# A retention layer and an MLP mixer in one kernel: the planner is given new durations, and the order and the engines of all steps are searched anew

## The chip, the cores and the metric

The kernel runs on one core of a Trainium2 chip. The metric is the time of one execution on the device in microseconds; of several runs the median is taken. Five engines work side by side: TensorE (PE, its weight loads shown apart as PEld), VectorE (DVE), ScalarE (ACT), GpSimd (POOL) and SyncE (SP). Each takes its instructions in the order in which the program lists them, and waits at an instruction until what it needs is there. Transfers are asked for by an engine (here GpSimd, SyncE and ScalarE) and then run on the DMA engines by themselves.

## The reference

```python
# q, k, v: (4, 8, 768, 64); B batches, H heads, S steps, D wide
gamma = 1.0 - 2.0 ** (-5.0 - np.arange(H))
for t in range(S):
    state = gamma * state + np.einsum('bhd,bhe->bhde', k[:, :, t], v[:, :, t])
    y[:, :, t] = np.einsum('bhd,bhde->bhe', q[:, :, t], state) / np.sqrt(D)
x = y.transpose(0, 2, 1, 3).reshape(B, S, H * D)                  # (4, 768, 512)
h = np.maximum(x.transpose(0, 2, 1) @ w_tok1, 0.0) @ w_tok2       # (768, 256), (256, 768)
u = x + h.transpose(0, 2, 1)
out = u + np.maximum(u @ w_ch1, 0.0) @ w_ch2                      # (512, 1536), (1536, 512)
```

## The kernel before

**The work.** A batch has four pairs of heads, and each pair goes through a *front* (`front`). Its k and q (loaded as fp16 by GpSimd's DMAs, L490 and L493) are scaled by powers of gamma (L531, L533) and turned, so that the head's width lies on the partitions: on TensorE (L555, L557, copied out at L565 and L570) for batches 0 and 1, by a DMA transpose from SyncE's queue (L545) for batches 2 and 3. A sequence is cut into six chunks of 128 steps. TensorE makes k by v of each chunk (L587), VectorE adds these up with decay (L599) and the result is scaled into `cross` (L617, L619). TensorE makes the scores of k and q (L638), VectorE masks them (L649, `am`), TensorE multiplies by v (L669) and adds what the earlier chunks give (L695). The sum leaves PSUM as x (L711), then follow the two token products (L726 with wt1, a relu at L735 or L737, L746 with wt2), whose result is added to x where it lies in PSUM, and leaves as u in fp16 and as X in fp32 (L711 twice). u is turned too (L791 and L797, or a DMA transpose).

Each batch then has a *back*: the product with wc1, a relu, the product with wc2, and the sum with X, which is stored (L1081, L983). Batch 0's first product is plain (`widen`, L825, L841). The others (`widen7`, L894; `narrow7`, L1042, L1052) multiply two by two blocks with seven products in place of eight; they need differences of blocks, which VectorE makes: of the weights once (`wsum` of wc2 at L1147, `AS` of wc1 at L1160, shown as `late`), of the activations each time (L864, L1006). Products that are used twice are kept in SBUF (`us`, L905, L1032), and the results come together at L914, L943 and L1059. The last blocks of batch 3 are done plainly in `narrow` (L968, L977).

**The order.** All this is 1246 steps, objects of `Op`, made in a fixed sequence and numbered so. A step has one or more *ways*: an engine, the time that it holds the engine, and the time until its result is there. Two strings written out in the kernel say what becomes of them. `ORDERED` lists all steps in the order of the plan, two characters for the number of each in base 62. `WAYS` has a digit for each step: which way it takes. From both each engine's own list follows, and that is what the engine is given. `arrange` walks through the lists with a model of the engines and the DMA rings (`Rings`, where `land` says how long after its last packet a transfer counts as landed), and gives each PSUM bank and buffer its place. The times of this walk aren't executed; they choose banks, and they decide how many *fillers* (matmuls of zeros, L1187, to keep TensorE running) stand between steps that are planned apart in the first 21 us. A search, outside the kernel, made the strings for these durations.

**Lists that the change touches.** GpSimd asks for q, k, v and the weights: wt1 (L473) as its step 11, the two halves of wt2 as 13 and 14, four parts of wc1 as 22, 23, 24 and 27, three parts of wc2 as 29 to 31. VectorE has the four sums of wc1 as steps 77, 87, 91 and 98, those of wc2 as 93 to 96, and batch 1's first mask as 66. The first pair's K comes in fp32 through SyncE, and both its halves are scaled on VectorE (L533). SyncE has 47 steps: one load, 26 DMA transposes and 20 stores; ScalarE issues the other stores.

Of the kernel before, what the change touches and what calls it, by code (L numbers as in the profile page):

```python
# [40 lines left out]
class Rings:  # L41
# [71 lines left out]
def arrange(ops, BANKS, seq, ways):  # L113
# [144 lines left out]

DIGITS = "0123456789abcdefghijklmnopqrstuvwxyzABCDEFGHIJKLMNOPQRSTUVWXYZ"
ORDERED = (  # L260
    "0d09060c070g010b000e0305080f1g0a1h0h1k0l1i1l0m1j0j1u1Q1v1R1y0i1w1U1x1S1V1T0n1m1n1z25241o280k2q1p272r1q0o2u1r"
    "262s1s1A291B0p1t342v2t1D350q1W1C1X2E1E1Y2F2H0v301Z2b20312G1F21322I222a2J0s1G23332d1H3e0u2c3h2w2e3g2x2f0w1I2y"
    "2z2K1J3f2A2B0r1L1K3j2L2C3i2g1M2D0t362h1N2M2N371O2O380x2i392P3k3a2l2j3b2Q1P3c0z3d5j2R4K2m0C2k483m3l493n3o2S2n"
    "2V3p4L0y4a2T3q2W2U0A2o3A3r2Y3B2p4b3v0B3s2Z3C5k3t3E2X0G4c3w3Fac3y3Daf0E3zai3xadaM4daeaNaPaQ3uaj0FagaYahauakav"
    "aZaO0Daxaw3Ob0aRaS3P0HaT3QayaUao3Saz3G3R4e3H4m4f3Ial4nap0I4g3JamaG4paqaHan3KaA1c0PaIaraD3LaE023MaB4has4iaCaJ"
    "4oatbd4qaKaF0Kbg4G4H4jb73NaLb14k1dbhbebi3Tbabmbf3U4l3W0Lbo3Vb43XbnaVb81f3Ybbb94rb2bcbp4Ib34tb50N184J3ZaW1940"
    "0Jbjb6bkaX1a41bO420M1bbl4443bq45bP1e4U464Mbrbx4v4V6m4Wbv4N5fbs4Obwby044P4s5g4Y4ubB0O4w4Q4Xbz4R0RbI4S5hbt4xbA"
    "4T5i0QbEbK5ObC50520T5P4y4ZbD6p51bT53c40S4z6nbFc8bU4A544C4BbX6qc54D6r5UbJc95l5V55bu4E5W5Rc7bM5m5X56bY5Scd5n5Y"
    "bN5o5a5T6U5Z5pbR5q60bQce5t6V5QbSbL575r5vch5s5u47bVci5x585y5w5AbWcm6o5bbZ5C5z5B0V6scn5Dc0c6596t5c5E6u616v5d6w"
    "c15Fcf6X6x4F6Y5e7s62cg7t5G646Z5J5Hcj635I65ca5K6W666y67ck695M5Lcb686b6a5N0X6A6ccl706z6E6d0U6Ccucq6ecI0Ycccwcv"  # L270
    "cr6icJ6f116Dcy6g6BcMczdCcs14cK6hcxcBcNcAct0WcCcPcLcOcQcDcG0Z71cW6jcRcEcHcU6kcFcS16cYcXcT6F6G6I72dD83127y736H"
    "cVcZd06JdG74157zd2d16KdIdHd37A75dJ7Bd46L7C7vdK7Dd5d86MdEdL76d6dFdOdMd7dPdodNd9da6N777w80787xdbdp6Q6O79de6R7b"
    "ds7udfdc7adqdt84dh6P7cdg859681dvdrdi7d7fdu8Bdwdj827e7h7gdmdx136SdA7idddkc28ydy17dlco7jdndzbGdB866l7kec7G7E97"
    "eged7F7o7Ieh7leeeE7m7H99el7K8C877L88dW7peF89em7N7Jencp9Eefepeo7n8a7Meyereq109adXeu8b8zez7O7Peiev7QeAeC7qesdQ"
    "7R7reDejdUet7S8Dek8edRdVeH8c8i8A7T8h8deJ8geI7U8f7W6TeLeK7XdS8k7Y8jdT7Z8leNeM8ndYeG8m8EeOc39ceBdZ989d8o9HeP9F"
    "eQ8F9ee0e19b8G7V9f8He3eR9ge2bH8p8Ie49heUe58q8JeVe88Ke68r8Le9eYe78s8MeZfc8N8tf28O8ufdf0f38Pfg8v8Qf5fh8xf19kf6"
    "eWfj8wfa9lew9GfefkeX8Rfb8Tfi9n8Vfo9mex9i8S8Uflf4fpfEff8Wfq9j9ofm8Xf7fnf88YfGfFf99qfsfH8ZfrfI90ftfufJ9pfv9K9I"
    "fL9Lfx9JfM9M9r9s9NfK919t92fy9OfwfN93fQfz9ufC95fO949PfRfAfDfSfP9veSfBfTg69wfWg79SfXga9W9xgb9UfZ9yfY9Tgdg09Vgc"
    "9zg4ge9Q9Xg8g1g5fU9Rg9gi9Agfgj9Yg2fV9Za0h2h6a1h4gga2goghhdh3h7h8hegGhbg3hhh5a3h9hcgqgHa4hihf9BgIa59DhggKhaa6"
    "hjhkgLhmgMgka8grgPgmhlgRglgQgpgvgna99CgSgtaba7gJgVgwgugTgNgWgxgsgUgOgzgygXgYgAgChogBhshGhphthIhqhHhuhwhvhKhx"  # L280
    "hygZhLhUhrhzhJhNhAiAgDhOhMhBgFi8eThPebhEaahChnhQgEhDhWhShRhViehFi9hYh0iahXhZicibhTi0i1idiCi2ifimi3igiGi6ihi4"
    "i7iki5iiioinijjAiliqiBisiriEiDjBipiFitjQiHiujeiIivjIiJjJiwiMixiyiNiKiziSiLjCjajKjLiOjfjDjcjEiPjMjliTjbiXiRiU"
    "jmiYiQjjjNjpjkiViZjdjOjnj0jPjqj1eajoh1jFjrj2j3jGjsj6iWjHj4jRjgj7j5j9jujSjhjxj8jvjYjTjijZjUjwjVjyk0k1k2jWjtk3"
    "jzk4jXk5"
)
WAYS = (
    "000000000000000000000000000000000000000000000000000000000000000000000000000000110000010000000000000000000000"
    "001000000000010000000000000000000100000100000000010000000000000000000000100001000100000000110000000000000000"
    "100101110100010000010000000000000000000011010000000000000000000000000100000100000000000100000000000000000000"
    "110000001000000000000000000000000001010000010000000000000000000000000000000000000000000000000010000000000100"  # L290
    "100100000000000000000000000000000110000000000000000000000000000011011000000000000000000000000000000001000100"
    "000000000000000000000000010000010000000000000001001000010000010001000000000000000010000000000000000000000000"
    "000000000000000000000000000000000000000000000000000000000000000000000000000011000000000000000000001100000000"
    "000000000000100000000000000000000000000000000000000000000000010000000000000000000000000000000000000000000000"
    "000000000000001100000000000000000000010000000000000000000010000000000000000000000000000000000000010000000000"
    "000000000001000001000000000000000010000000000000001000100000110000000000000000000001000000000010000000001100"
    "000000000000000000000000000000000000000000000100000000000100000000000001000000000000000000010000000000000001"
    "0000000000100010000100100000000001000000010000000000000001"
)


# [1 line left out]
def kernel(  # L303
# [22 lines left out]
    SH = S // 2  # L326
# [55 lines left out]
    def either(emit, **costs):  # L382
        return [(e, c[0], c[1], lambda emit=emit, e=e: emit(e)) for e, c in costs.items()]
# [98 lines left out]
    def load(b, p, what):  # L482
        src = dict(k=k, q=q, v=v)[what][b, 2 * p:2 * p + 2]
        hard = (b, p, what) in HARD
        wide = what == "q" and TURN[b, p, "q"] == "w"
        s = Slot("us" if hard else what)

        def emit():
            if wide:
                nc.gpsimd.dma_start(out=tile_of(s, [P, 2, NC, D], F16).rearrange("p h c d -> p h (c d)"),  # L490
                                    in_=src.rearrange("h (p c) d -> p h (c d)", c=NC))
            else:
                (nc.sync if hard else nc.gpsimd).dma_start(out=tile_of(s, [P, 2, NC, D], FP if hard else F16),  # L493
                                                           in_=src.rearrange("h (c p) d -> p (h c) d", p=P))
        dma = (96, 17) if hard else (16, 66) if wide else (96, 13.5)
        if hard:
            o = Op(ops, (-20, 0, b, p), [("SP", 500, 500, emit)], [], [s], dma=dma)
        else:
            o = request((-20, 0, b, p), 710 if wide else 1030, emit, dma, [s])
        loads[b, p, what] = (s, o)  # L500

    def front(b, p):
# [22 lines left out]
        def decayed(tag, src, dep, g, hard):  # L525
            dst, got = Slot(tag), []
            for j in range(2):
                def emit(e, j=j):
                    t, h = opened(dst, [P, NC, 2, D], F16)[:, :, j], 2 * p + j
                    if e == "ACT":  # L530
                        nc.scalar.activation(t, src.tile[:, j], AF.Copy, scale=g[:, h:h + 1])  # L531
                    else:
                        (nc.vector if e == "DVE" else nc.gpsimd).tensor_scalar(t, src.tile[:, j], g[:, h:h + 1], None,  # L533
                                                                               ALU.mult)
# [56 lines left out]
        prev = None  # L591
# [18 lines left out]
        if pair:  # L610
            rs = []
            for j in range(2):
                def emit(e, j=j):
# [3 lines left out]
                        nc.scalar.activation(r, u, AF.Copy, scale=g)  # L617
                    else:
                        nc.vector.tensor_scalar(r, u, g, None, ALU.mult)  # L619
                rs.append(op(either(emit, ACT=(455 + 115 * j, 555 + 40 * j), DVE=(465, 545)), [prev, cross_op] + rs, [] if j else [RS],  # L620
                             [RS, US] if j else [US]))
        else:
            rs = [op(either(emit, ACT=(455, 555), DVE=(305, 390)), [prev], [RS], [US])]
# [14 lines left out]
                nc.tensor.matmul(SC[g].tile[:, i * P:(i + 1) * P], KT.tile[rows, t], QT.tile[rows, t],  # L638
                                 start=True, stop=True)
# [165 lines left out]
    def back(b):  # L805
# [10 lines left out]
        def widen(sh):  # L816
            H2 = H2s[sh]
            rel = []
            for ft in range(NF):
# [17 lines left out]
                def emit(e, ft=ft, A=A, H2=H2):  # L837
# [382 lines left out]
```

## Time and profile before

| what | us |
|---|---|
| median of 3 runs | 186.37 |
| lowest and highest | 186.11, 187.1 |
| the profiled execution | 186.01 |
| its span, first to last instruction | 184.2 |

A page of the profile gives each engine's busy time as a share of the span, and the chain that ended last: from the last instruction back, at each step to what released it. A group's row names line, engine, operation, output and inputs, count, then busy time and mean nanoseconds of one, then the idle time ahead of it and what ended it. A row of a stretch gives the busy time of each engine in that stretch. A matmul's end is modelled and matmuls overlap, so TensorE's busy time says little by itself; the distance from one start to the next says more. The granted clock of TensorE was 0.998.

### The profile page before, as it was taken

The numbers are of one execution on the slowest core, as the hardware profiler recorded it, in microseconds if no ns is written. First come the engines' busy times: TensorE is split into PE (matmuls) and PEld (weight loads), VectorE is DVE, ScalarE is ACT, GpSimd is POOL, SyncE is SP. The second block draws the span as 40 slices with busy tenths as digits, with TensorE's granted clock in tenths as the row PEclk, the third lists the DMA queues.
The fourth block names the chain that finished last, engine by engine and source line by source line (L and its number), as shares of the span: only waits on it lengthen the run. The fifth ranks groups of instructions, "written<-read, shape, count | busy, mean of one in ns | idle before, by whom it ended". The sixth has DMA issues, their size and how long they took to land.

```text
span 184.2 us, 5242 instructions
## 1 busy us (share of the span) xinstructions
PE 176.4 (96%) x2087; PEld 134.1 (73%) x2087; DVE 166.0 (90%) x420; ACT 126.4 (69%) x295; POOL 53.6 (29%) x63
## 2 busy tenths in 40 slices
PE   7898999999999999999999999999999999999990
PEld 3465798566789788867669889677679986566880
DVE  5799899599999999999989999998999899779891
ACT  3858796659988999888998786989651516671000
POOL 8995776463409102595040200000000000000000
PEclk9999999999999999999999999999999999999999
DMA  6999999999999999999979998073400321700093
GB/s 109 155 172 179 188 177 201 179 194 206 167 156 142 157 110 159 137 149 155 136 143 243 207 141 205 30 197 33 113 0 4 101 43 68 278 0 0 4 342 115
DMA packets 94137, 25.31 MB, mean 137 GB/s; under 512 B 83616, under 2 KB 91296, under 8 KB 94112
## 3 DMA queue, kind: packets, MB, share of 16 engines
q0 software_dynamic: 67728, 13.18, 86.6%
q1 hardware_dynamic: 25232, 10.10, 26.9%
q10 hardware_dynamic: 1152, 1.70, 2.7%
q8 instruction: 16, 0.26, 0.6%
q14 instruction: 9, 0.07, 0.2%
HBM read 26.74 MB, written 6.29 MB: 179 GB/s over the span
## 4 chain that ended last, share of the span: by engine, by line
PE 65%; DMA 18%; DVE 7%; POOL 5%; issue 1%; POOLq 0%; DVEq 0%
PE bank L894 23%; PE bank L1042 14%; DMA wc<-in_moe_w_ch_dram 14%; PE bank L1052 10%; DMA wt<-in_moe_w_tok_dram 5%; PE bank L726 4%; PE bank L746 4%; PE bank L638 2%; PE bank L968 2%; DVE wsum L1147 2%; POOL q L490 2%; DVE X L1059 2%; PE bank L669 2%; PE bank L695 2%; POOL k L493 2%; PE bank L587 1%
## 5 line engine op out<-in xcount | busy, mean ns | idle before, releaser
L649 DVE TENSOR_TENSOR am<-bank,mask 128x384 f16<-128x384 f32 x64 | 32.6, 552 | 3.7 <-PE bank L638 3.7
L914 DVE CUSTOM_DVE_ANT_0 h<-bank,us 128x384 f16<-128x384 f32 x54 | 28.2, 554 | 3.6 <-ACT us L905 1.7
L905 ACT COPY us<-bank 128x384 f32<-128x384 f32 x49 | 22.7, 485 | 9.3 <-PE bank L894 6.0
L493 POOL DMA_DIRECT2D v<-in_v_dram x16 | 16.5, 1029 | 40.1 <-PE bank L695 20.7
L894 PE MATMUL bank<-hs,late 128*128 128x384 f16 x108 | 22.2, 326 | 0.0
L1032 ACT COPY us<-bank 128x256 f32<-128x256 f32 x27 | 10.0, 377 | 16.3 <-PE bank L1042 13.7
L1042 PEld LDWEIGHTS <-hs 128*128 128x128 f16 x192 | 18.3, 98 | 2.1
L894 PEld LDWEIGHTS <-late 128*128 128x128 f16 x144 | 13.3, 98 | 7.9 <-DVE hs L864 0.2
L1059 DVE TENSOR_TENSOR X<-X,bank 128x256 f32<-128x256 f32 (+1 forms) x45 | 18.1, 411 | 0.5 <-PE bank L1052 0.2
L599 DVE SCALAR_TENSOR_TENSOR U<-U,gp,bank 128x64 f32<-128x64 f32 x64 | 17.3, 284 | 1.1 <-ACT U L597 0.4
L617 ACT ACTIVATE cross<-U,gp 64x320 f16<-64x320 f32 x28 | 15.7, 560 | 3.0 <-DVE U L599 2.7
L1042 PE MATMUL bank<-wsum,hs 128*128 128x256 f16 x132 | 17.5, 273 | 0.0
L825 PE MATMUL bank<-uT,wc 128*128 128x384 f16 x96 | 17.1, 326 | 0.0
L894 PE MATMUL bank<-uT,wc 128*128 128x384 f16 x72 | 16.1, 326 | 0.0
L493 POOL DMA_DIRECT2D k<-in_k_dram x15 | 15.3, 1035 | 2.5 <-ACT x L711 0.9
L711 ACT CAST u<-bank 128x384 f16<-128x384 f32 x30 | 14.5, 492 | 1.3 <-PE bank L746 1.1
L746 PE MATMUL bank<-h,wt 128*128 128x128 f16 x192 | 15.2, 219 | 0.0
L894 PEld LDWEIGHTS <-wc 128*128 128x128 f16 x108 | 10.1, 98 | 6.1 <-issue 0.7
L711 ACT CAST x<-bank 128x384 f16<-128x384 f32 x29 | 13.7, 489 | 0.9 <-PE bank L695 0.7
L746 PEld LDWEIGHTS <-wt 128*128 128x128 f16 x192 | 12.4, 98 | 2.1 <-DMA wt<-in_moe_w_tok_dram 0.6
L1052 PEld LDWEIGHTS <-h 128*128 128x128 f16 x132 | 12.4, 98 | 2.0 <-issue 0.6
L841 ACT ACTIVATE h<-bank 128x384 f16<-128x384 f32 x24 | 10.4, 494 | 4.9 <-PE bank L825 4.7
(92 smaller groups left out, 376.0 us busy)
## 6 DMA issues: line engine op xcount, KB each, us to landing
out_dram<-X SPq DMA_DIRECT2D x16, 256.0 KB, 2.7
q<-in_q_dram POOLq DMA_DIRECT2D x16, 192.0 KB, 6.9
v<-in_v_dram POOLq DMA_DIRECT2D x16, 192.0 KB, 6.9
k<-in_k_dram POOLq DMA_DIRECT2D x15, 192.0 KB, 7.0
wc<-in_moe_w_ch_dram POOLq DMA_DIRECT2D x5, 512.0 KB, 13.5
out_dram<-X ACTq DMA_DIRECT2D x6, 256.0 KB, 2.7
wc<-in_moe_w_ch_dram POOLq DMA_DIRECT2D x2, 256.0 KB, 8.6
us<-in_k_dram SPq DMA_DIRECT2D x1, 384.0 KB, 3.5
```

The source lines that it names most:

```text
L493: (nc.sync if hard else nc.gpsimd).dma_start(out=tile_of(s, [P, 2, NC, D], FP if hard else F16), in_=src.rearrange("h (c p) d -> p (h c) d ...
L599: nc.vector.scalar_tensor_tensor(out=u[:, c], in0=u[:, c - 1], scalar=gp[:, p:p + 1], in1=st, op0=ALU.mult, op1=ALU.add)
L649: nc.vector.tensor_tensor(am, SC[g].tile[:, :m * P].rearrange("p (i t) -> p i t", t=P), mask.to_broadcast([P, m, P]), ALU.mult)
L711: (nc.scalar.copy if e == "ACT" else nc.vector.tensor_copy)(tile(), t)
L746: nc.tensor.matmul(Y[j].tile[:, 2 * i * D:2 * (i + 1) * D], wt2[:, jt, t], H1.tile[:, jt], start=False, stop=(jt == NJ - 1), skip_group_ch ...
L825: nc.tensor.matmul(acc[:, :SH], wc1[:, ct, ft * P:(ft + 1) * P], UT.tile[:, ct, sh * SH:(sh + 1) * SH], start=(ct == 0), stop=(ct == NP - 1))
L894: nc.tensor.matmul(acc[:, :SH], left(ct), r[:, ct], start=first and ct == 0, stop=ct == C2 - 1, skip_group_check=True)
L905: (nc.scalar.copy if e == "ACT" else nc.vector.tensor_copy)(ks[:, j], R1.tile[:, :SH])
L914: nc.vector._custom_dve(TENSOR_ADD_SAT, out=h(m, sh), in0=R.tile[:, :SH], in1=KS.tile[:, j], s0=TOP, s1=0.0)
L1042: nc.tensor.matmul(acc_[:, lo], l[:, j], r[:, j], start=first and j == 0, stop=j == K2 - 1, skip_group_check=True)
L1052: nc.tensor.matmul(acc_[:, lo], l[:, j], r[:, j], start=first and j == 0, stop=j == K2 - 1, skip_group_check=True)
L1059: (nc.vector if e == "DVE" else nc.gpsimd).tensor_tensor(dst(), dst(), b_(), ALU.add)
```

## The change

The planner's durations are changed at seven places, and the two strings are replaced. No step is added or taken away.

```diff
     def land(self, q, op, t):
         if q == "POOL":
-            return 1470 if t < 4500 else 2100 if t < 26000 else 1700
+            return 1470 if t < 4500 else 2100 if t < 26000 else 1700 if t < 50000 else 2200
         if op.dma[0] == 48:
-            return 1300 if t < 115000 else 900
-        return 900
+            return 1800 if t < 115000 else 1500
+        return 1200
...
-        dma = (96, 17) if hard else (16, 66) if wide else (96, 13.5)
+        dma = (96, 17) if hard else (16, 66) if wide else (96, 13.5 if b < 2 else 14.1)
...
-                got.append(op(either(emit, ACT=(506, 610), DVE=(340, 420) if hard else (600, 690) if b == 0 else (231, 312)),
+                got.append(op(either(emit, ACT=(517, 615), DVE=(840, 920) if hard else (600, 690) if b == 0 else (300, 380)),
...
-                rs.append(op(either(emit, ACT=(455 + 115 * j, 555 + 40 * j), DVE=(465, 545)), [prev, cross_op] + rs, [] if j else [RS],
+                rs.append(op(either(emit, ACT=(468 + 102 * j, 562 + 33 * j), DVE=(465, 545)), [prev, cross_op] + rs, [] if j else [RS],
...
-            k_ = 165 * len(run) // 2
+            k_ = (178 if len(run) == 2 else 330)
...
-                rel.append(op(either(emit, ACT=act(SH)),
+                rel.append(op(either(emit, ACT=act(SH, 0, 0.5)),
...
-    "0d09060c070g010b000e0305080f1g0a1h0h1k0l1i1l0m1j0j1u1Q1v1R1y0i1w1U1x1S1V1T0n1m1n1z25241o280k2q1p272r1q0o2u1r"
+    "0d07060c0109000g0308050b0e0f1g1h0i0a1k0h1i1l1j0l1u1Q1R0m1v1x0j1U1w1S1V1T0n1m1y1n241o1A27250k301z311p26320o2q"
...
```

Read step by step, the two pairs of strings differ in this. Of TensorE's 446 steps all stay, in another order; the array changes its shape (whole, split by rows, split by columns) between neighbours 68 times instead of 64. GpSimd asks for wc1's parts as steps 18, 22, 23 and 24; what stands ahead of wt1, of wt2 and of wc2 is the same set as before in another order. VectorE has the sums of wc1 as steps 62, 63, 66 and 68, those of wc2 as 90, 92, 93 and 95, and batch 1's first mask as 69. 69 steps go from VectorE to ScalarE or back: of the scalings of k and q ten leave VectorE (one of them the second half of the first pair's K) and five come to it. Twelve stores change between SyncE and ScalarE; SyncE has 45 steps, and a store of batch 0 stands ahead of the transposes of pair 3 of batch 2.

More of the change, by code (lines that the diff above doesn't have):

```diff
@@ L266 @@
[L266 to L270, printed above, removed]
@@ new lines @@
+    "1J2A3e2B0s1L1K3i2g2C3h3g2D2K0v361M2L372N2h2M381O1N0x392i2O3a3E3b2P3c2l2j0C2Q3d2k2m1P3k3m2R3l3F3n3o0B2o2S3p2p"
+    "2V3q0u2T3A2W4c3r0G3B4K4d3s2X2Y0A3t3v2Z3C3w5j0y3u3x3yal2n3zac3Daf4LadaM0D5kaeb7aoaYagaNamaZaOauanav0F1cahaJ2U"
+    "bgawaK1dbh0E48bab1aL02b249aA0I1eb3aBb0arasbi4a0Hatbb4baCaxaybc1f3O0MazaD3Pap3RaEaqai3SaFaj3Q4G4m4H0J3Gak4n4e"
+    "b84f3HaG3Ib9aH4q4I4gaIaV3J4J3T3Kbd4h0L3LaW4p3Mb44ob53NaPbmaQb64ibjbnaR3Vbebo3X3U3W18aXaS0KaTbfbk3Y4j1absaU0N"
+    "043Zbl190Pbq40bt4k1b4Mbr4U4l414Xbv5f0Q4V5g444N4Y4r42bxbI0Rbw434O4s4u4W454tbz4P4vbJ0O5h4w4QbObybAbp5ibB4RbP4S"
@@ new lines @@
+    "4xbL5O4TbE4ybC466p4Z514z5R53bF50525Pc44C0Xc854c55QbD5lc95U4A55bK475V4B5mcd5n6U565obT4D5pce5WbMbu4EbU6m575X5S"
+    "bNbX5Y6q5T5q5ZbR5rbY58c75t6r5sbSch5v6n5ubVci6o5w595abW5xcm5bc64F5y5AbQ5z5B5Ccf0Scn5D5d5c7sc00Ucg6V5e5E60c10T"
+    "bZ625F616s640W5G6t635J5Hca6u655K67665I696v5L5Mcb686b6w6acj5N0V6c6xcq6A6y16ck6d7t6Ccucc6e0YcIcl6zcwcr6icv0Z6f"
+    "cJ6Ecy6g6BcMczcW6DcKcNcscB6XcPcLcCcActcQcOcDcG6hcU6YcHcEcR6Z6jcYcF6F6kcScx6HcVdC6WcT6JdEdDdI7v6G80cX6IdFdG12"
+    "co6Kd0817udH70cZ7yd1dJ717w726L6l73dK7z74d3756MdOdLd4d27x7AdP6N7BdMd56OdadNd66Pd87Cdbd7dod96Q83dpde84827D786R"
@@ new lines @@
+    "dfds767adcdt79dh8ydqdddvdi7bdg6Tdwdu7c777ddmdjdA85dxdn7edkdBdr107f7g6SdleEbH7hec117G7ieF7Edy7H7j147Fdz7J867k"
+    "dW8z177I7KeidX7L877Ney7M7O7P7l1388ejeg7Qed7m7o8915ehef7R7n8ael8b967S8cee8eem7T978iep7p8fenez7req7U8h7W7qeueo"
+    "c28A8g7VereA7XeveC8BdQ7YdUeseDek8d8jdSeH8Cet8k8m8l8DdReJdVeIeB9EdZeK7Z99dTeLe0dY9aeNeG8neM9b8EeO9ceQ8F9d8GeP"
+    "9Hcpe18o9e988He39f8Ie28peRe4bGc38Je59g8qeU9Ie89heV8K8re6eYe98se78MeZfc8L8Pf28N8ufdf0f38Ofg8t8Qf5fhf19kf6eWfj"
+    "8vfa9nfk8xf4eX8w8Rfof7fb8Tfifp9m8S8U8Vflf8fE8Wf9fe9Ffm9ofF8X9Gff9i9lfIfqfnfJewfseTfK9JfrfL8Y9j9qftfufGfM8Zfv"
@@ L285 @@
+    "jjiTiZjmjGiXjkjHjpjdiYj0jnjOiRj1jPjojqh0j3jrj2eSiUj4jsj6j5jgiVj8j7jQiWjujhjRk0j9jSk1jTjik2k3jUjvjVjxjtk4jwjW"
+    "k5jyjXjz"
 )
 WAYS = (
[L287 to L290, printed above, removed]
@@ new lines @@
+    "000000000000110000000000000000000000000000000000000000000000000000000000000000000000000000000000000000000000"
+    "000000000000000100000000000000000000110000000000000000000010000000000000000000000000000000000100000000000100"
+    "000000000000000000000000000000000010000000000100000000100000110000010000100010000011000000000000000000001000"
+    "000000000000000000000000000001000001000000000000000000000000000000100000000000000000000000010000000000000000"
+    "0000010000100000001100000100000000000000010000000000000001"
```

39 lines of the change are left out of this document (13 added, 26 removed).

## The prediction

> **What bounds the kernel now.** I read the busy table first, then the chain of work that ended last, the stretches of ten microseconds, and last the waits of TensorE.
>
> ```profile
> PE 176.4 (96%) x2087; PEld 134.1 (73%) x2087; DVE 166.0 (90%) x420; ACT 126.4 (69%) x295; POOL 53.6 (29%) x63
> ...
> PE 65%; DMA 18%; DVE 7%; POOL 5%; issue 1%; POOLq 0%; DVEq 0%
> ```
>
> ```profile
> 9.56 8.59 DMA wt<-in_moe_w_tok_dram
> ...
> 32.04 16.22 DMA wc<-in_moe_w_ch_dram
> 48.35 0.97 DVE wsum L1147
> ...
> 60.73 0.67 DVE X L1059 x2
> 61.44 0.81 PE bank L1052 x6
> ...
> 70.28 0.67 PE bank L726 x12
> 70.95 0.34 PE bank L791 x6
> ...
> 151.66 10.80 PE bank L894 x66
> ```
>
> ```profile
> 30.00:40.00 10.00, 10.00 (x120) 6.25 (x121) 7.67 (x17) 5.17 (x14) 5.01 (x7) 1.00 1.72 187
> 40.00:50.00 10.00, 10.00 (x95) 6.77 (x94) 9.64 (x20) 9.10 (x21) 4.95 (x5) 1.00 1.58 191
> 50.00:60.00 10.00, 10.00 (x142) 8.98 (x141) 9.94 (x23) 8.68 (x22) 4.45 (x5) 1.00 2.36 150
> 60.00:70.00 10.00, 9.54 (x142) 8.18 (x141) 9.96 (x29) 9.41 (x26) 1.03 (x2) 1.00 1.79 139
> 150.00:160.00 10.00, 10.00 (x68) 6.40 (x66) 8.81 (x19) 5.50 (x13) 0.00 (x0) 1.00 0.42 159
> ```
>
> Columns of the last: stretch, sum, then PE, PEld, DVE, ACT, POOL, clock, DMA share, GB/s. The reader is to see three regimes. Up to 48 us the chain goes through weight loads. From 48.35 to 61.4 it is VectorE, filled to 9.94 of 10. From 61.44 to the end it is TensorE, one step behind the other.
>
> A busy TensorE isn't yet a full one, so I count its work by spacing: 66 matmuls of 384 columns in 10.80 us are 164 ns each, twelve of L726 take 0.67. Summed so over the 23 groups of matmuls but the fillers of L1187 (first and last quoted), the plan's 446 steps need 158.9 us.
>
> ```profile
> L894 PE MATMUL bank<-hs,late 128*128 128x384 f16 x108 | 22.2, 326 | 0.0
> ...
> L1187 PE MATMUL bank<-zero 128*128 128x384 f16 x35 | 9.3, 401 | 1.1 <-DVE zero L1178 1.1
> ...
> L1095 PE MATMUL bank<-wc,hs 128*128 128x128 f16 x12 | 0.9, 219 | 0.0
> ```
>
> A change of the array's shape (whole, rows split, columns split) costs time too. L726 above starts 0.67 before the next step; where the next is L587, split by columns, it is 0.76:
>
> ```profile
> 95.11 0.83 PE L726 MATMUL bank<-x,wt 128*128 128x128 f16 x12
> 95.87 0.35 PE L587 MATMUL bank<-v,k 128*64 128x64 f16 x10
> ...
> 178.64 1.17 PE L968 MATMUL bank<-wc,h 128*128 128x128 f16 x18
> ```
>
> So 0.09 there, 0.09 to 0.11 at all switches by the same subtraction. The order of before has 64 of them: 7.0 us, and 165.9 of work in all. Call the start of a step less the work ahead of it its **lateness**. The last two matmuls start 0.90 after 178.64, with 165.8 ahead: 13.7 late. Lateness never falls, and every rise is a wait. By the same count it is 11.6 at 18.20, 12.3 from 22 to 57 us, 12.9 at 61.44, 13.5 from 98 on. So all that any order can win behind 18.2 us is these 2.1 us.
>
> **The change, part by part.** The program's instructions stay the same in kind and size; what moves is read off the two strings, step by step.
>
> *New numbers of the planner.* They run nowhere on the chip. They act through the order, and through the 35 fillers of the first 20 us (401 ns each at most, only where TensorE is planned idle). A filler more or less costs between -0.4 and 0.4 and is behind the loads' gates below; I take 0.
>
> *TensorE's order.* It has 68 switches instead of 64: two more visits to the row-split shape, four times 0.10, **+0.4 us**, all on the path. The work is 166.3.
>
> *The loads' gates.* Three waits show where weights set the pace:
>
> ```profile
> 18.20 0.67 PEld L726 LDWEIGHTS <-wt 128*128 128x128 f16 x12 [0.28 <-DMA wt<-in_moe_w_tok_dram]
> ...
> 21.36 0.34 PEld L746 LDWEIGHTS <-wt 128*128 128x128 f16 x6 [0.20 <-DMA wt<-in_moe_w_tok_dram]
> ...
> 34.32 1.42 PEld L825 LDWEIGHTS <-wc 128*128 128x128 f16 x10 [0.24 <-DMA wc<-in_moe_w_ch_dram]
> ```
>
> GpSimd asks for both wt2 halves behind the same set of loads as before, so they land as before. At 21.36 the order of before had 9.14 us of work ahead, the changed one has 9.28: lateness 12.1 instead of 12.2. wc1's parts move from GpSimd's steps 22, 23, 24, 27 to 18, 22, 23, 24:
>
> ```profile
> 22.03 1.58 POOL L473 DMA_DIRECT2D wc<-in_moe_w_ch_dram  x2
> 23.88 0.74 POOL L473 DMA_DIRECT2D wc<-in_moe_w_ch_dram  x1 [0.27 <-DMA q<-in_q_dram]
> ...
> 27.34 0.76 POOL L473 DMA_DIRECT2D wc<-in_moe_w_ch_dram  x1
> ```
>
> ```profile
> DMA to landing us min/median/max: 8.3/12.0/16.2
> ```
>
> The second view is that of the tile wc. With the median of 12 us the last part landed at 39.3. It now has three loads fewer ahead; at 150 GB/s (stretch 50 to 60) one of 192 KB takes 1.3 us, so it lands near 35.4. Its first matmul now has 23.5 us of work ahead (27.4 before): lateness at least 11.9. The part at 34.32 loses one load and has 20.9 ahead: 33.0, lateness 12.1. Together the gates give 12.1 to 12.2 instead of 12.3: **-0.1**. wc2 is asked for behind the same set in both, so 48.35 stays.
>
> *VectorE's sums.* This is the main term.
>
> ```profile
> 36.43 1.95 DVE L649 TENSOR_TENSOR am<-bank,mask 128x384 f16<-128x384 f32 x4 [2.27 <-PE bank L638]
> ...
> 40.29 0.95 DVE L1160 TENSOR_TENSOR late<-wc 128x1536 f16<-128x1536 f16 x1
> ...
> 44.42 0.96 DVE L1160 TENSOR_TENSOR late<-late,wc 128x1536 f16<-128x1536 f16 x1
> ...
> 52.28 0.95 DVE L1160 TENSOR_TENSOR late<-wc 128x1536 f16<-128x1536 f16 x1
> ```
>
> Four masks of 0.55 fill 1.95, so a step holds VectorE 0.09 less than its duration: 0.86 for a sum of wc1. These four stand at VectorE's steps 77, 87, 91, 98 and go to 62, 63, 66, 68, ahead of batch 1's first mask, where VectorE sat idle for 2.27. So 3.4 us leave the full stretch, one of them from behind the wsum sums. Further, ten k and q scalings go to ScalarE and five come back; with all other exchanges VectorE has 1.8 us less work and ScalarE 2.1 more.
>
> ```profile
> L531 ACT ACTIVATE k<-k,gk 128x384 f16<-128x384 f16 x19 | 11.3, 615 | 0.4 <-DMA k<-in_k_dram 0.3
> ...
> L533 DVE TENSOR_SCALAR k<-k,gk 128x384 f16<-128x384 f16 x11 | 3.9, 368 | 0.0
> L533 DVE TENSOR_SCALAR k<-us,gk 128x384 f16<-128x384 f32 x2 | 1.9, 936 | 0.6 <-ACT gk L416 0.6
> ```
>
> ScalarE, 69% busy, hides that; uncovered it would cost the 2.1. Now add VectorE's steps from wc2's landing at 48.35 to each result that TensorE needs, and subtract the work ahead. Before, the worst is the L1059 ahead of 61.44: 12.75 us of steps, 48.5 ahead, lateness 12.6 (it was 12.9, with this wait):
>
> ```profile
> PE bank L1052 <- DVE X L1059: 0.5, 1, 0.5
> ```
>
> In the changed order that pair has 14.85 and 51.9: 11.4. The worst is the fourth wsum: 52.5, 40.5 ahead, 12.0. That is below the loads' 12.2, so this rise of 0.6 should go; I take **-0.5**. The small rises from 61 us on (12.9 to 13.7) fall where VectorE is at 9.96; half of them, **-0.4**, may go as it has more room.
>
> *The start.* The second half of K of the first pair goes from VectorE (0.94) to ScalarE, behind L436:
>
> ```profile
> 4.30 2.49 ACT L436 ACTIVATE late<-us,lnsc,lnh 128x384 f32<-128x384 f32 x4
> ```
>
> It starts near 6.8 then and takes some 0.6. Its scores come some 1.1 us later. The cover is wt1's landing: TensorE has only 6.5 us of work ahead of 18.20 in both orders. Without that cover it costs 1.1.
>
> *Stores and transposes.* Twelve stores swap SyncE for ScalarE or back, and SyncE's order of transposes and stores changes. The first transpose pair queued behind a store now is pair 3 of batch 2: its store waits for a VectorE step near 76.6, its k and q are scaled near 82, its scores are due near 94. Cost 0; if the store were 10 us late, the excess. ScalarE issues two stores more, and behind one that waits for its VectorE add stand evacuations; with 31% of ScalarE idle I take 0, at most the 0.4 of an issue each. The end keeps its form, last matmul, 128-column add, 64 KB store: 0 (bounds -0.1 and 0.3).
>
> *New waits.* The trace can't show those of an order that hasn't run. From below 0; from above what the order of before collected behind 22 us, 1.4. I take 0.2, since the largest waits of before are where the new order has more room.
>
> Sum: 0.4 - 0.1 - 0.5 - 0.4 + 0.2 = **-0.4 us**. The profiled execution took 186.01, of it 1.8 outside the span of 184.2, 0.36 under the median of 186.37. The forecast is 185.6 against that execution, and 0.45 under the median: **185.9**.
>
> *Two rules of the Trainium skill.* The rows first: in the stretch 150 to 160 weight loads fill 6.40 of 10, while the matmuls stand 164 ns apart without a gap. The Trainium skill, "Perfetto Trace Analysis", Identifying the Most-Contended Engine, says to judge TensorE's headroom by the busy share of its weight loads, not of its matmuls. By that rule 27% of the span would be free and a new order could win far more; by the spacing only the waits are free. Second, GpSimd's issues beside VectorE's sums:
>
> ```profile
> 48.78 1.01 POOL L493 DMA_DIRECT2D q<-in_q_dram  x1 [1.60 <-DMA wc<-in_moe_w_ch_dram]
> ...
> 58.54 1.04 POOL L493 DMA_DIRECT2D q<-in_q_dram  x1
> ```
>
> The first starts among the wsum sums and isn't longer than the second. The Trainium skill, "SBUF — State Buffer", Who interferes with whom, says that a VectorE operation with two inputs in SBUF contends with GpSimd's reads. By it the sums moved to 35 us could hold up requests.
>
> **Rivals.** *Slower: wc1's sums come before their data.* VectorE takes its steps in order, so batch 1's scaling, its k evacuation and its first masks now queue behind the sums, and the sums behind the last part of wc1. My 35.4 is an estimate. From a landing near 36.5 on, each microsecond later is one more on all of VectorE's full stretch, hence on TensorE. At 37.7 that makes +1.2, and the -0.5 and the -0.4 don't come: 187.3 to 187.6. For it: a load's request to landing varies, 8.3 to 16.2 us for wc. Against it: the part moves three loads forward. Requests held by a sum would end here too, by up to 0.95 each. Chance 0.17.
>
> *The room is hidden.* The waits are only moved: some other result is late at each place, and the switches remain. 186.37 + 0.4 - 0.1 is 186.7, within 0.5%. For it: lateness 12.1, 12.2 and 12.0 come from three unlike causes, so removing one uncovers the next. Chance 0.2.
>
> *All waits go.* TensorE runs from 22 us on without one: 166.3 + 12.2 against 165.9 + 13.7 is -1.1, so 185.2. Chance 0.16. *TensorE isn't the bound*, several microseconds to win, 183 or less: the spacing speaks against it, chance 0.02.
>
> **How the numbers follow.** Forecast 0.45, with its own range 185.4 to 186.3. About 0.5% (0.93 us) is what a measurement of this kernel can tell from no change: 185.44 and 187.30 are the marks. Faster by more: 0.16 + 0.02 and a sixth of the forecast, 0.26. Slower by more: most of the slower rival and some ends of the hidden one, 0.18. Within: 0.56. The range takes in the case without waits and the slower one up to 187.5.
>
> **What would show it.** L1160 stands near 35 to 39 us, ahead of batch 1's masks, and VectorE's idle 2.27 is gone; the wait of L1052 on L1059 near 61 is gone; a wait of L825 on wc of 0.3 or less near 33 to 36. Wrong it would be if TensorE waits on VectorE between 36 and 60 us, if t1 starts later than 18.6, if a wait on kT or qT of batch 2 or 3 over 0.5 shows, or if ScalarE ends a wait of TensorE over 0.5.

## The result, and the profile after

| | before | changed |
|---|---|---|
| median | 186.71 us (15 runs, 184.98 to 187.76) | 185.37 us (15 runs, 184.34 to 187.08) |
| ratio | | 0.9934, 95% interval 0.9905 to 0.9963 |
| repeated | 186.97 us (35 runs) | 185.41 us (12 runs), ratio 0.9944, 0.9912 to 0.9977 |
| profiled execution, its span | 186.01, 184.2 | 184.34, 182.6 |

The change makes the kernel 1.3 us faster by the medians, 0.66% by the ratio. The forecast was 185.9, a gain of 0.45, and the gain is three times that. The whole range, from the case without waits (185.2) to 187.5, holds 185.37; the forecast's own range ends at 185.4, and a result past the mark of 185.44 had been given a chance of 0.26. The sum behind the forecast fails where it counts, as the end of this part and the experiments show.

The page of the changed kernel, first the busy time, then the chain's shares by engine:

```profile
PE 175.7 (96%) x2086; PEld 133.5 (73%) x2086; DVE 165.7 (91%) x421; ACT 128.9 (71%) x294; POOL 53.5 (29%) x63
...
PE 80%; DVE 7%; POOL 5%; DMA 5%; issue 1%; ACT 0%; POOLq 0%; ACTq 0%
```

TensorE holds 80% of the chain instead of 65%. The waits of TensorE (engine, line, what ended the wait; total, times, longest):

```profile
PE bank L555 <- DMA q<-in_q_dram: 1.1, 1, 1.1
PE bank L557 <- ACT k L531: 0.5, 2, 0.3
PE bank L638 <- ACT kT L570: 0.4, 2, 0.2
PE bank L726 <- DMA wt<-in_moe_w_tok_dram: 0.4, 1, 0.4
PE bank L638 <- DVE am L649: 0.2, 1, 0.2
```

The wait of L1052 on L1059 is gone, as forecast. VectorE's own row of time, around the sums of wc1:

```profile
32.25 1.81 DVE L565 TENSOR_TENSOR qT<-bank,late 128x768 f16<-128x768 f16 x2
35.57 0.96 DVE L1160 TENSOR_TENSOR late<-wc 128x1536 f16<-128x1536 f16 x1 [1.51 <-DMA wc<-in_moe_w_ch_dram]
36.56 0.96 DVE L1160 TENSOR_TENSOR late<-late,wc 128x1536 f16<-128x1536 f16 x1
...
40.01 0.56 DVE L570 COPY kT<-bank 128x768 f16<-128x768 f16 x1 [1.25 <-PE bank L557]
40.48 0.95 DVE L1160 TENSOR_TENSOR late<-wc,late 128x1536 f16<-128x1536 f16 x1
```

The sums stand where the two strings put them, and wc1's last part is there at 35.57 (the estimate was 35.4). But VectorE's idle time isn't filled: it has become a wait of 1.51 for that part and one of 1.25 for TensorE. Its stretches of ten microseconds (sum, PE, PEld, DVE, ACT, POOL, clock, DMA share, GB/s):

```profile
30.00:40.00 10.00, 10.00 (x87) 6.51 (x85) 6.83 (x11) 7.04 (x16) 4.92 (x6) 1.00 1.85 182
40.00:50.00 10.00, 10.00 (x116) 6.43 (x115) 9.87 (x26) 8.52 (x20) 2.93 (x3) 1.00 1.58 190
50.00:60.00 10.00, 10.00 (x156) 9.15 (x154) 9.94 (x25) 9.44 (x23) 5.15 (x6) 1.00 2.69 155
60.00:70.00 10.00, 10.00 (x143) 8.79 (x141) 9.89 (x29) 8.85 (x23) 1.65 (x2) 1.00 1.68 126
```

VectorE is as full from 40 us on as it was. Where, then, do the 1.6 us come from by which these two spans differ? The end of both kernels, from the last matmuls on, first before:

```profile
179.58 0.56 DVE L977 TENSOR_TENSOR X<-X,bank 128x128 f32<-128x128 f32 x2
180.13 0.39 ACTq L983 DMA_DIRECT2D out_dram<-X  x1
180.51 0.34 SPq L983 DMA_DIRECT2D out_dram<-X  x1
```

and changed:

```profile
179.16 0.49 PE L1095 MATMUL bank<-wc,hs 128*128 128x128 f16 x6
179.41 0.36 SPq L983 DMA_DIRECT2D out_dram<-X  x1
179.64 0.34 ACTq L983 DMA_DIRECT2D out_dram<-X  x1
179.69 0.29 DVE L1059 TENSOR_TENSOR X<-X,bank 128x128 f32<-128x128 f32 x1
180.01 0.33 SPq L1081 DMA_DIRECT2D out_dram<-X  x1
```

A matmul of 128 columns takes 0.22 (the row of L1095 in the prediction). The last one starts at 178.64 + 1.17 - 0.22 = 179.59 before, and at 179.16 + 0.49 - 0.22 = 179.43 in the changed kernel. TensorE is done only 0.15 earlier. The span ends 4.6 us behind that start before, and 3.1 after: **the gain lies behind the last matmul**, which the prediction had put at 0.

Two things are to be seen there. Before, VectorE's last result is there at 179.58 + 0.56 = 180.14, ScalarE issues its store at 180.13, and SyncE issues its own only at 180.51. In the changed kernel the result is there at 179.98 and SyncE issues at 180.01. And the packets, by queue, in two stretches of before (queue and kind: packets, MB, share), 181.2 to 181.8 and 181.8 to 184.2:

```profile
q1 hardware_dynamic: 135, 0.06, 35.1%
q10 hardware_dynamic: 112, 0.05, 29.0%
q14 instruction: 1, 0.01, 6.5%
...
GB/s 0 0 0 0 0 0 0 17 26 17 17 9 17 17 17 0 0 0 0 0 0 0 0 0 0 0 0 0 0 0 0 0 0 0 0 0 0 0 0 0
...
q1 hardware_dynamic: 9, 0.00, 0.8%
q10 hardware_dynamic: 9, 0.00, 0.6%
```

The stores' packets are through by 181.8, but for eight of 512 bytes on each queue (the ninth is a small one). Those come one after the other, as one DMA engine would send them: the row of GB/s has slices of 0.06 us, and shows them from 182.22 to 182.70. Between them and the others stands the packet on q14: 8 KB of instructions, 181.62 to 182.24 by its record in the trace. Below it is called the fetch. In the changed kernel the fetch comes when all is sent; this is the stretch 181.25 to 182.6:

```profile
DMA packets 1, 0.01 MB, mean 6 GB/s; under 512 B 0, under 2 KB 0, under 8 KB 0
## 3 DMA queue, kind: packets, MB, share of 16 engines
q14 instruction: 1, 0.01, 2.4%
```

### The profile page after: what moved, and what is told of

Same layout as the page of the kernel before. It is cut to its first block, busy times and chain, and to the rows that moved or that the text cites. A ratio compares the mean times of both kernels' runs of the same rounds, so it can differ in the third digit from the quotient of the medians.

```text
span 182.6 us, 5244 instructions
## 1 busy us (share of the span) xinstructions
PE 175.7 (96%) x2086; PEld 133.5 (73%) x2086; DVE 165.7 (91%) x421; ACT 128.9 (71%) x294; POOL 53.5 (29%) x63
## 4 chain that ended last, share of the span: by engine, by line
PE 80%; DVE 7%; POOL 5%; DMA 5%; issue 1%; ACT 0%; POOLq 0%; ACTq 0%
PE bank L894 22%; PE bank L1042 14%; PE bank L1052 11%; PE bank L825 9%; PE bank L746 5%; DMA v<-in_v_dram 5%; PE bank L726 5%; PE bank L638 3%; PE bank L968 3%; PE bank L669 2%; PE bank L695 2%; PE bank L587 2%; DVE X L1059 2%; POOL k L493 2%; POOL q L490 2%; DVE U L599 1%
## 5 line engine op out<-in xcount | busy, mean ns | idle before, releaser
L914 DVE CUSTOM_DVE_ANT_0 h<-bank,us 128x384 f16<-128x384 f32 x54 | 29.0, 555 | 3.2 <-PE bank L894 1.8
L894 PE MATMUL bank<-hs,late 128*128 128x384 f16 x108 | 22.8, 326 | 0.0
L894 PEld LDWEIGHTS <-late 128*128 128x128 f16 x144 | 12.9, 97 | 7.6 <-issue 0.3
L1059 DVE TENSOR_TENSOR X<-X,bank 128x256 f32<-128x256 f32 (+1 forms) x45 | 18.0, 412 | 0.1
L1032 ACT COPY us<-bank 128x256 f32<-128x256 f32 x24 | 8.9, 374 | 13.1 <-PE bank L1042 12.8
L894 PE MATMUL bank<-uT,wc 128*128 128x384 f16 x72 | 16.1, 326 | 0.0
L711 ACT CAST u<-bank 128x384 f16<-128x384 f32 x28 | 13.5, 490 | 3.0 <-PE bank L746 2.8
L711 ACT CAST x<-bank 128x384 f16<-128x384 f32 x30 | 13.7, 493 | 2.1 <-PE bank L695 2.0
L531 ACT ACTIVATE k<-k,gk 128x384 f16<-128x384 f16 x23 | 13.7, 616 | 0.8 <-DMA k<-in_k_dram 0.7
L841 ACT ACTIVATE h<-bank 128x384 f16<-128x384 f32 x24 | 10.9, 493 | 4.2 <-PE bank L825 4.0
L746 PEld LDWEIGHTS <-wt 128*128 128x128 f16 x192 | 12.3, 98 | 1.9
L894 PEld LDWEIGHTS <-wc 128*128 128x128 f16 x108 | 9.9, 98 | 5.3
```

What stands on the lines that cost most here:

```text
L711: (nc.scalar.copy if e == "ACT" else nc.vector.tensor_copy)(tile(), t)
L746: nc.tensor.matmul(Y[j].tile[:, 2 * i * D:2 * (i + 1) * D], wt2[:, jt, t], H1.tile[:, jt], start=False, stop=(jt == NJ - 1), skip_group_ch ...
L894: nc.tensor.matmul(acc[:, :SH], left(ct), r[:, ct], start=first and ct == 0, stop=ct == C2 - 1, skip_group_check=True)
L914: nc.vector._custom_dve(TENSOR_ADD_SAT, out=h(m, sh), in0=R.tile[:, :SH], in1=KS.tile[:, j], s0=TOP, s1=0.0)
L1059: (nc.vector if e == "DVE" else nc.gpsimd).tensor_tensor(dst(), dst(), b_(), ALU.add)
```

## The experiments

"The last matmul" below is its start, "the end" the time from there to the end of the span, both worked out as above. Lateness is counted as in the prediction. Steps are named by their numbers.

### Both kernels again, and the end exchanged

Both kernels once more as they are, and two mixtures: steps 1078 to 1245 (batch 3's back) take the order and the engines of the other kernel, in the places that these steps had.

```diff
-    seq = [digit[a] * 62 + digit[c] for a, c in zip(ORDERED[::2], ORDERED[1::2])]
+    seq, way_of = mix(decoded(ORDERED), [int(x) for x in WAYS], set(range(1078, 1246)))
...
+def mix(seq, ways, part):
+    other, theirs = decoded(OTHER), [int(x) for x in OTHER_WAYS]
+    new = iter([i for i in other if i in part])
+    return [next(new) if i in part else i for i in seq], [theirs[i] if i in part else w for i, w in enumerate(ways)]
```

> The kernel before once more, for a second profile. In the first profiles the last matmul starts at 179.59 (before) and 179.44 (changed), 0.15 apart, but the span ends 4.6 and 3.2 us behind it. 'The middle' (the gain comes from the waits of TensorE, and the long end of before was one late packet by chance): the distance from the last matmul's start to the span's end is 3.2 to 3.9 here, and the last matmul starts near 180.4, as much later as the medians differ. 'The end' (the order of the last stores is worth over 1 us): the distance is 4.3 or more again, the last matmul starts near 179.6.

> The changed kernel once more, for a second profile. 'The middle': the last matmul starts near 179.4 with a lateness of 13.1 at the end, against 13.7 or more before, distance to the end 3.2 to 3.9. 'The end': the distance is 3.0 to 3.4 and shorter than that of before by over 1 us, while the last matmuls of the two kernels start within 0.3. Time 185.3, 0.993 of before.

> The kernel before, with the steps of batch 3's back alone (1078 to 1245, the last 35 us) in the order and on the engines of the change. 'The end': 185.4, distance from last matmul to the span's end about 3.2. 'The middle': no change, 186.4 to 186.8; the wait of L1052 on L1059 near 61 us and the lateness of 12.9 behind it stay, at most the 0.2 of before's rise from 13.5 to 13.7 can go.

> The changed kernel, with the steps of batch 3's back alone in the order and on the engines of before. 'The end': 186.5, distance from the last matmul to the span's end 4.3 or more. 'The middle': 185.4 to 185.7, lateness 12.4 at 61 us and no wait of L1052 on L1059 there; at most 0.2 is given back at the end.

| kernel | median us | ratio to before, interval | last matmul | the end |
|---|---|---|---|---|
| before, again | 186.97 | 0.9999, 0.9965 to 1.0034 | 179.6 | 4.3 |
| changed, again | 185.41 | 0.9944, 0.9912 to 0.9977 | 179.9 | 3.2 |
| before with the new end | 185.51 | 0.9940, 0.9905 to 0.9976 | 179.7 | 3.1 |
| changed with the old end | 186.09 | 0.9967, 0.9937 to 0.9996 | 180.6 | 3.6 |

"The end" holds: before with the new end alone has the whole gain. "The middle" falls: in the two profiles of each kernel the last matmul starts at 179.6 and 179.6 before, 179.4 and 179.9 changed. These four executions are all faster than their kernel's median, by 0.5 to 1.4 us, so they don't show what a slower one waits for; the mixture with the new end, whose median has the whole gain, doesn't depend on them. Only the last mixture fits neither theory, since its end of 3.6 lies between. It has 46 steps on SyncE, where before has 47 and the changed kernel 45, and its fetch comes at 182.8, behind the last store's packets. So I took the fetch for SyncE's own, asked for at a fixed place of its list.

### SyncE's list made shorter and longer

Two kernels in which only stores far from the end change their engine. Before, with two of them moved to ScalarE:

```diff
+    for i, ahead in ((1077, 1126), (879, 1105)):
+        seq.remove(i)
+        seq.insert(seq.index(ahead), i)
...
-    total, order, start, end = arrange(ops, BANKS, seq, [int(x) for x in WAYS])
+    way_of = [{1077: 0, 879: 0}.get(i, int(x)) for i, x in enumerate(WAYS)]
+    total, order, start, end = arrange(ops, BANKS, seq, way_of)
```

and the changed kernel with 878, 1077 and 923 moved to SyncE in the same way.

> The kernel before with two of its stores (batch 1's at 155.7 us, batch 2's at 156.2) issued by ScalarE, 25 us ahead of the end; SyncE has 45 steps instead of 47, and the last stores stay as they were. 'Code fetch': the 8 KB packet on the instruction queue that starts at 181.6 and 181.3 in the two profiles of before is SyncE's, asked for at a fixed place in its list, and holds eight packets of each of the last two stores on one DMA engine. Two steps fewer move it behind the last store: the last packet lands 1.1 us behind its issue instead of 1.8 to 2.2, the span ends 3.5 to 3.7 us behind the last matmul instead of 4.3 to 4.6, and the time is 0.7 to 1.0 less, near 186.1. 'Order of the last stores': the end stays at 4.3 to 4.6 and the time at 186.9.

> The changed kernel with three stores (batch 1's at 123.6 and 140.8 us, batch 2's at 148.8) issued by SyncE; it has 48 steps instead of 45, the last stores stay as they were. 'Code fetch': the fetch now starts some six of SyncE's instructions earlier, near 180.6 to 181.0 instead of 181.7 and 182.4, while the last store's packets (180.9 to 181.2) are due: some of them come 0.3 to 0.7 later, and the span ends 3.4 to 3.9 behind the last matmul instead of 3.1 to 3.2; time 185.7 to 186.1. 'Order of the last stores': 3.1 to 3.2 again, 185.4.

| kernel | SyncE's steps | median us | ratio to before, interval | the end |
|---|---|---|---|---|
| before, two stores fewer | 45 | 186.52 | 0.9971, 0.9928 to 1.0014 | 3.6 |
| changed, three stores more | 48 | 185.94 | 0.9971, 0.9936 to 1.0006 | 4.0 |

Both ends move as "code fetch" says, the second by a little more, though nothing at the end was touched. The queue q14 carries other engines' code too: in the first profile two of its packets, at 33.7 and 57.2 us, come while SyncE stands between the same two steps. That the last one is SyncE's follows from the two kernels: VectorE's and GpSimd's lists are unchanged in them, and ScalarE's grows by two stores where the fetch comes later and shrinks by three where it comes earlier, so a fetch of its code would have moved the other way. Of before with 45 steps, the last rows of VectorE and of the two queues:

```profile
181.51 0.55 DVE L977 TENSOR_TENSOR X<-X,bank 128x128 f32<-128x128 f32 x2
182.06 0.39 ACTq L983 DMA_DIRECT2D out_dram<-X  x1
182.09 0.33 SPq L983 DMA_DIRECT2D out_dram<-X  x1
```

SyncE's store follows VectorE's result (182.06) by 0.03, not by 0.37, and from 183.75 to 185.2 the fetch is the only packet. Of the changed kernel with 48 steps:

```profile
180.45 0.34 ACTq L983 DMA_DIRECT2D out_dram<-X  x1
180.50 0.29 DVE L1059 TENSOR_TENSOR X<-X,bank 128x128 f32<-128x128 f32 x1
181.12 0.33 SPq L1081 DMA_DIRECT2D out_dram<-X  x1
```

Here the store waits 0.33 behind its result (180.79), although SyncE's store before it was issued by 180.58, and eight of its packets come behind a fetch of 182.04 to 182.39. So SyncE's place in its code costs twice: a pause of 0.33 to 0.37, and the wait of the packets behind the fetch, the last of which ends 0.3 to 1.0 behind all others. That the pause belongs to the fetch is read from their coming together: of the 14 profiles of this case six have both, and in the other eight SyncE's last store follows its result by 0.02 to 0.03 and no packet of a store stands behind the fetch.

The times say less than the ends. Before with 45 steps was to gain 0.7 to 1.0; it gained 0.1 by the medians and 0.5 by the ratio, with an interval that reaches 1.0014. Its profile shows why it needn't come: a new wait of TensorE of 1.4, near 96 us.

```profile
PE bank L894 <- DVE h L914: 1.4, 1, 1.4
```

The same wait stands in the profile of a kernel below whose SyncE is unchanged ("before, sums narrow"). Its cause is a row of VectorE in that profile, and the kernel with 45 steps has the same row with 1.99:

```profile
94.21 0.32 DVE L533 TENSOR_SCALAR q<-q,gy 128x384 f16<-128x384 f16 x1 [2.00 <-DMA qT<-q]
```

The scaling of q writes a buffer that a DMA transpose still reads, and VectorE's whole list waits for the transpose. In the seven profiles that have the middle of before, VectorE waits so for 0.4, 0.5, 0.6, 0.8, 1.2, 2.0 and 2.0, and TensorE's lateness rises between 90 and 100 us by 0.2 to 1.7. Where the middle is the changed one, no scaling on VectorE waits for a transpose and the rise is below 0.1.

### The sums of wc1 moved

The changed kernel with the four sums back at before's places, before with the sums and wc1's parts early, and the changed kernel with two sums late. All three edits are lists of steps and of the step they are put ahead of:

```diff
+    for i, ahead in ((74, 232), (75, 70), (77, 71), (76, 308)):
...
+    for i, ahead in ((35, 30), (37, 34), (30, 34), (74, 216), (75, 216), (76, 237), (77, 237)):
...
+    for i, ahead in ((77, 71), (76, 308)):
```

> The changed kernel with the four sums of wc1 back at VectorE's steps 77, 87, 91 and 98. 'VectorE's sums count': lateness 12.9 or more at 62 us, with a wait of L1052 on L1059 of 0.4 to 0.6 near there where no load has made TensorE late before; the time is 0.3 to 0.5 longer than that of the changed kernel, 185.8 to 186.0. 'The loads hide them': in the profiles so far the lateness at 62 us is 12.7, 12.9 and 13.0 with the order of before ahead of it and 12.4, 12.9 and 13.0 with the changed one, so a load's wait near 30 to 40 us takes the room; then no change beyond 0.2, 185.4.

> The kernel before with wc1's last two parts asked for at GpSimd's steps 18 and 24 and the four sums at VectorE's steps 65 to 69, ahead of batch 1's first mask; all else is as before. 'VectorE's sums count': no wait of L1052 on L1059 near 61 us, lateness there 12.3 to 12.5; the time is 0.3 to 0.5 less, 186.5. 'The loads hide them': lateness 12.7 to 13.0 at 62 us by a wait on wc or another load near 30 to 40 us, time 186.9. The slower rival (the sums come ahead of their data): TensorE waits on VectorE at 36 to 60 us, 187.3 or more. The span's end stays 4.2 to 4.7 behind the last matmul.

> The changed kernel with two of the four sums of wc1 moved from VectorE's steps 66 and 68 to 91 and 98: 1.7 us of work go from its idle time into its full stretch, half of what the run with four late sums moved (that took 3.5 us more than the changed kernel). By adding up VectorE's steps as in the prediction, its lateness goes from 11.4 to 13.1, against 12.4 to 13.2 that the loads leave: between 0 and 0.7 more, 185.4 to 186.1. If instead each microsecond of VectorE counted in full: 1.7 more, 187.1.

| kernel | median us | ratio to before, interval |
|---|---|---|
| changed, four sums late | 188.93 | 1.0127, 1.0077 to 1.0177 |
| changed, two sums late | 186.69 | 1.0033, 1.0005 to 1.0062 |
| before, sums and parts early | 200.32 | 1.0731, 1.0683 to 1.0780 |

All three miss what I expected. Four sums late cost 3.5 over the changed kernel's 185.4 (by the ratios 3.4), two cost 1.3 (by the ratios 1.7). Four sums hold VectorE for 3.4 and two for 1.7: nearly every microsecond put into VectorE's full stretch counts. The profile with two late shows where TensorE pays:

```profile
57.82 0.82 PE L1052 MATMUL bank<-wc,h 128*128 128x256 f16 x6 [0.33 <-DVE am L649]
59.00 0.60 PE L1052 MATMUL bank<-wsum,h 128*128 128x256 f16 x4 [0.36 <-DVE X L1059]
```

Its lateness goes from 13.0 at 50 us to 14.6 at 62. The two waits and one of 0.3 on L1059 near 53 us name 1.0 of these 1.6; the rest is in waits that the view doesn't name. By my sum it was to be 13.1 there.

The 14 us of the third kernel have nothing to do with sums:

```profile
38.25 0.55 DVE L533 TENSOR_SCALAR k<-k,gk 128x384 f16<-128x384 f16 x2 [10.73 <-DMA k<-in_k_dram]
```

To bring wc1's last part forward I had put a load of k (step 30) behind it. In before VectorE scales that k at its steps 50 and 51, ahead of all that matters, and stands for 10.73. In the changed order ScalarE has the first half, and VectorE the second at its step 65. The moves of the load, the scalings and the sums belong together; taken one by one they can't be priced in this way.

### The sums taken away, and the last steps alone

To bound what VectorE's work on the sums costs, wherever they stand, both kernels with the sums over 16 of 1536 columns and L894 fed with wc1 itself:

```diff
-                        return lambda ct: AS.tile[:, j, ct, i * P:(i + 1) * P]
+                        return lambda ct: wc1[:, ct, i * P:(i + 1) * P]
...
-            nc.vector.tensor_tensor(AS.tile[:, j], x(), y(), f)
+            nc.vector.tensor_tensor(AS.tile[:, j, :, :8], x()[:, :, :8], y()[:, :, :8], f)
```

and before with only the last steps exchanged, by the same `mix` over 1188 to 1245.

> The kernel before, with the four sums of wc1 made over 16 of their 1536 columns, and L894 multiplying with wc1 itself in their place: that part of the output is not the reference's. The order stays; VectorE has some 3.2 us less to do in its full stretch. It bounds from above what any place for the sums can bring. 'VectorE sets TensorE near 61 us': the wait of L1052 on L1059 (0.5 in the first profile) goes, lateness at 62 us 12.3 to 12.7, time 0.3 to 0.6 less, near 186.3. 'The loads hide it': lateness at 62 us 12.7 to 13.0 without that wait, no change beyond 0.2, 186.7.

> The changed kernel with the same cut (the sums over 16 columns, L894 with wc1 itself; output not the reference's). 'The changed order has room on VectorE': no change beyond 0.2, 185.4; lateness at 62 us set by the loads, 12.2 to 13.0. 'VectorE still bounds': 0.4 or more less, 185.0.

> The kernel before, with the last steps alone (1188 to 1245: the last two block rows of batch 3, their adds and stores) in the order and on the engines of the change; SyncE keeps 47 steps. 'Code fetch and order, each its own part': SyncE still pauses 0.4 before its last store and the fetch still holds packets: the span ends 3.5 to 4.0 behind the last matmul, against 4.3 to 4.6 before and 3.1 with the changed end and a shorter list; time 0.4 to 0.8 less than before. 'The order alone does it': 3.1 to 3.2, time 1.2 less.

| kernel | median us | ratio to before, interval | the end |
|---|---|---|---|
| before, sums narrow | 186.28 | 0.9998, 0.9966 to 1.0030 | 4.1 |
| changed, sums narrow | 185.19 | 0.9940, 0.9906 to 0.9974 | 3.1 |
| before, last steps new | 188.69 | 1.0130, 1.0075 to 1.0186 | 5.2 |

With 3.2 us less on VectorE neither kernel is faster than it was. Of before's, the stretch from 40 to 50 us:

```profile
40.00:50.00 10.00, 10.00 (x95) 6.77 (x93) 7.62 (x21) 9.01 (x22) 5.05 (x5) 1.00 1.60 190
```

VectorE falls from 9.64 to 7.62, and the wait near 61 us is gone (lateness 12.3 at 62 us). But the time isn't less: this profile has the 2.0 and the 1.4 shown above, and the interval leaves room for 0.6 at most. So **what the sums' place could bring is small**, and below what the other waits make of it. (The narrow sums stand where the full ones stood and still wait for wc1, so it is their work that is taken away, not such a wait.)

The last mixture fails as an experiment on the order. The new last steps don't fit the old ones ahead of them: TensorE waits 1.1 for L1032, VectorE's last result comes 1.1 behind the last matmul's start instead of 0.5. What it shows again is the fetch, with SyncE's 47 steps and other last stores; the stretch is 185.35 to 187.6:

```profile
DMA packets 10, 0.01 MB, mean 5 GB/s; under 512 B 1, under 2 KB 9, under 8 KB 9
## 3 DMA queue, kind: packets, MB, share of 16 engines
q14 instruction: 1, 0.01, 0.9%
q1 hardware_dynamic: 9, 0.00, 0.8%
```

Eight packets of the last store come behind the fetch here too, and SyncE issues that store 0.47 behind its result (183.48, issue at 183.95).

## Why the prediction was right, and where it wasn't

That the time lies in the range is luck: the term put at nothing brings the gain, and the two that were to bring it, VectorE's relief and the small rises, brought little. Term by term:

**The end, put at 0 (bounds -0.1 and 0.3): -1.2.** This step failed, and it is nearly all of the result. "The end keeps its form, last matmul, 128-column add, 64 KB store" looked at the instructions and not at what else uses SyncE and the DMA engines there. Nor did the bound of 2.1 us on "all that any order can win" hold: it counts the waits of TensorE, and they end at the last matmul. The old end takes 4.1 to 4.6 us with 47 steps on SyncE (four profiles) and 3.6 with 45 or 46 (two); the new one 3.1 to 3.2 with 45 or 46 (five) and 4.0 with 48. So some 0.7 of the 1.2 is SyncE's code, which the change moves by having 45 steps, and some 0.5 is the order of the last stores. The times split in two as well, though each interval alone is wide: with the new order and the fetch out of the way the ratios are 0.9934, 0.9944 and 0.9940, with one of the two alone 0.9967 and 0.9971 (old order, 46 and 45 steps) and 0.9971 (new order, 48 steps). That the 0.5 comes from stores that stand too close together is only argued. For it: the times from issue to landing of the last stores, of before with 45 steps

```profile
DMA to landing us min/median/max: 1.6/2.0/2.1
```

and of the changed kernel:

```profile
DMA to landing us min/median/max: 1.6/1.8/2.1
```

The old order ends with two stores issued 0.03 apart. The new one issues its last store alone, 0.37 behind the one before it. By the records of the packets, the last one ends 1.54 and 1.55 behind the issue of SyncE's last store in the two kernels with the old order and the fetch out of the way, and 1.22 to 1.24 in the five with the new one; no run spaces the two old stores apart.

**The switches, +0.4: held.** The work counts 166.3 instead of 165.9, and it is paid: with lateness at the end lower by 0.55 in one pair of profiles and by 0.05 in the other (13.2 and 13.7, against 13.7 twice) the last matmul starts 0.15 earlier in the one and 0.35 later in the other.

**The loads' gates, -0.1: held at 22 us.** Lateness there is 12.1 twice, against 12.2 twice. The gate of wc1 near 34 us held in one profile only, as the next term shows.

**VectorE's relief, -0.5: the mechanism is there, the gain isn't.** The wait near 61 us goes where it was. But it stood in one of the two profiles of before only, and in the changed kernel's second profile a load near 34 us takes its place, with 0.6 of lateness (a wait of 0.3 was the most that the forecast allowed there):

```profile
PE bank L825 <- DMA wc<-in_moe_w_ch_dram: 0.4, 1, 0.4
```

Lateness at 62 us is 12.9 and 12.7 before, 12.4 and 12.9 changed. The working was wrong too. I added up VectorE's steps from 48.35 us as if its list were empty then, and found 0.9 of room for the adds ahead of L1052 (48.35 + 14.85 - 51.9 is 11.3, not 11.4, against the loads' 12.2) and 0.2 for the fourth wsum sum. In the changed kernel VectorE is busy for 9.87 of the ten us up to 50 and comes to the first wsum sum at 48.70, without a wait for wc2; two late sums showed that there is no room. With the sums taken away nothing is gained either, so loads, VectorE and TensorE end together here, which is the mechanism, though not the time, of the rival "the room is hidden".

**The small rises, -0.4: half.** The rise between 90 and 100 us, 0.3 and 0.5 in the profiles of before, is gone; a rise of 0.2 at 153 us and smaller ones are new. I had put it down to VectorE's fullness. It is a transpose, and I had looked at the transposes (under "Stores and transposes", cost 0) for their landing at TensorE, and not at the buffers that they read. This is worth up to 1.6 in some executions of before; in how many can't be said, since the times come without a profile, and the mixture with the new end, which keeps the wait, has the whole gain all the same.

**New waits, +0.2: about right** in size: 0.2 near 29 us in one profile, 0.6 near 34 us in the other.

The slower rival didn't come: the first sum could start at 35.6 in one profile and at 36.4 in the other, just short of the 36.5 from which it would have counted. The run with two late sums agrees with its price per microsecond. Nor did the sums hold up requests: GpSimd's issues beside them took 1.01 to 1.03 us, as long as elsewhere.

The Trainium skill, "Perfetto Trace Analysis", Identifying the Most-Contended Engine, judges TensorE's headroom by the busy share of its weight loads, beside its share of peak arithmetic (MFU). By the first of these a new order could have won far more; no run here started its last matmul earlier than 179.4. The Trainium skill, "Runtime: NRT & Kernel Launch", Instruction fetch mechanics, says that an engine fetches its next block of code through a DMA queue of its own while it runs the current one, and that crossing a block is mostly hidden. Here it was not, at the end of SyncE's list: 0.33 to 0.47 of pause, and packets that end up to 1.0 behind all others.

## What to carry to other kernels

Count the end of a kernel by itself, from the last matmul to the last landing: when 0.5% matters, a microsecond there is worth as much as one on the busiest engine, and here it depended on how many steps an engine off the critical path had issued. Where a buffer is written again, the transfer that reads it is a wait of the writer's whole list, so look for writers behind transposes. And VectorE, full to 9.9 of 10, had no room to give, though taking work from it brought nothing: test both ways.

## What the runs showed of the hardware

A fetch of 8 KB of SyncE's code shares the DMA engines with stores: in the six profiles in which it came ahead of the last packets (before twice; sums narrow; sums early; three stores more; last steps new), eight packets of 512 bytes of one or two stores stood behind its 0.31 to 0.68 us. Two or three steps more or fewer in SyncE's list decide whether that happens at the end. While a DMA transpose still reads a buffer, VectorE, which writes it next, waits: 0.4 to 2.0 with the same steps in its list up to there. How much of the 2 to 3 us over which the kernel's executions spread comes from this isn't shown: the changed kernel, without such a wait, spreads over 2.7 too.
